# Attention in an order written out for TensorE, ScalarE and VectorE, ahead of two mixtures of experts

## The chip, the core and the metric

The kernel runs on one core of one Trainium2 chip. Five engines work side by side, each through its own queue of instructions, in order: TensorE (PE in the profile) multiplies matrices and transposes, and writes to PSUM alone; VectorE (DVE), ScalarE (ACT) and GpSimd (POOL) work element by element; SyncE (SP) issues the DMA transfers. They meet through semaphores. The metric is the device time of one execution in microseconds (us).

## What is computed

Attention with four batches, eight heads, 1152 keys of 64, where two neighbouring queries are averaged (576 a head), then a mixture of eight experts whose gate is normalised by rows and columns eight times, then a soft mixture with 32 slots. The change is in the attention alone:

```python
def _attn_ref(q, k, v):
    q_pool = q.reshape(B, H, S // 2, 2, D).mean(axis=3)
    scores = (1 / np.sqrt(D)) * np.matmul(q_pool, k.transpose(0, 1, 3, 2))
    scores = scores - np.max(scores, axis=-1, keepdims=True)
    attn = np.exp(scores)
    attn = attn / (np.sum(attn, axis=-1, keepdims=True) + 1e-09)
    return np.matmul(attn, v)
...
    x = attn_out.transpose(0, 2, 1, 3).reshape(B * S, H * D)
    x = _moe_ref(x, ...)
    return _moe2_ref(x, ...)
```

## The kernel before

The attention goes through 16 pairs of heads. A pair has 1152 pooled queries; they make nine tiles of 128, in the order ORDER: first one tile that holds the last 64 queries of both heads (h = 2), then four of head 0 and four of head 1. The loop has one step a tile (NT = 144 tiles; s counts the nine steps of a pair, pi the pairs).

What a tile goes through. emit_SA makes its products with the first 768 keys (SA, two PSUM banks, two buffers) and VectorE takes their maximum (L183); emit_SB does the last 384 keys (SB, one bank, one buffer), the maximum (L191), and the negated maximum of both, nm (L192). emit_exp takes the exp on ScalarE, of SB (L202) and of SA (L203), with the sums on the side. emit_T transposes e in nine chunks of 128 on TensorE: part 0 (four chunks, copied out of PSUM by ScalarE), part 1 (four, by VectorE) and part 2 (the ninth; for the tiles of a head only at every second tile, two chunks at once), into etA, etB or etL. emit_PV multiplies nine chunks of a head by v into the PSUM tile o (one buffer), in two products a chunk (g), which write different halves of the partitions; h = 2 is etL. Every product with v is in full fp32 and stands in the trace as two records. emit_recip inverts the sums, emit_R turns them with transposes (rb, r), and emit_O multiplies o by them into x.

Beside it the next pair is made ready: k_bank transposes k and splits it into a coarse part (ScalarE, L124) and a rest (VectorE, L125), q_bank does the same with q, half after half (L107, L108); kd_dma copies k to both halves of the partitions; pool_q adds query neighbours on GpSimd. All transposes, of e, k, q and the sums, go through two PSUM banks (bank(), pool ps_t), which they use in turn.

In the stage of the attention the order on each engine is set by the framework's scheduler: the loop below gives the program order, and the scheduler lets an instruction that is ready pass one that is not. Products with v are cut by CS in the program into runs of two or three chunks in four steps, and the scheduler cuts them further. The experts after it stand in an order of their own, the program's.

Of the kernel before, what the change touches and what calls it, by code (L numbers as in the profile page):

```python
# [8 lines left out]
F32 = mybir.dt.float32  # L9
F32R = mybir.dt.float32r  # L10
AF = mybir.ActivationFunctionType
# [10 lines left out]
STEPS = len(ORDER)  # L22


def attention(ctx, nc, tc, q, k, v, xa, ident, hooks):
    B, H, S, D = q.shape
    raw_p = ctx.enter_context(tc.tile_pool(name="raw", bufs=2))
    kq_p = ctx.enter_context(tc.tile_pool(name="kq", bufs=1))
    r_p = ctx.enter_context(tc.tile_pool(name="r", bufs=2))
    e_p = ctx.enter_context(tc.tile_pool(name="e", bufs=4))  # L30
    sm_p = ctx.enter_context(tc.tile_pool(name="sm", bufs=4))
    v_p = ctx.enter_context(tc.tile_pool(name="v", bufs=2))
    et_p = ctx.enter_context(tc.tile_pool(name="et", bufs=1))
# [4 lines left out]
    NPAIR = len(pairs)  # L38
# [38 lines left out]
    def pool_q(pi, u):  # L77
        st = prep.setdefault(pi, {})
        if u == 0:
            st["qp"] = kq_p.tile([128, 9, 2, 64], F32, tag="qp", name="qp")  # L80

            st["qs"] = kq_p.tile([128, 1024], F32R, tag="qs", name="qs", bufs=2)
        qr = raws["q"][pi]
        eng = nc.gpsimd if pi else nc.vector
        eng.tensor_tensor(out=st["qp"][:, :, u, :], in0=qr[:, :, 0, :], in1=qr[:, :, 1, :], op=ALU.add)
# [27 lines left out]
    def k_bank(pi, c0, n, ps, at):  # L113
        st = prep.setdefault(pi, {})
        if c0 == 0:
            st["kp"] = kq_p.tile([128, 2, 1152], F32R, tag="kp", name="kp")
        kr = raws["k"][pi]
        for c in range(n):
            nc.tensor.transpose(
                ps[:, at + c * 128:at + (c + 1) * 128], kr[:, c0 + c].rearrange("p h d -> p (h d)"), ident  # L120
            )
        o = st["kp"][:, 0, c0 * 128:(c0 + n) * 128]
        s = ps[:, at:at + n * 128]
        nc.scalar.copy(o, s)  # L124
        nc.vector.tensor_tensor(  # L125
            out=st["kp"][:, 1, c0 * 128:(c0 + n) * 128], in0=s, in1=o.bitcast(F32), op=ALU.subtract
        )
# [34 lines left out]
    NT = len(tiles)  # L162
# [15 lines left out]
    def emit_SA(i):  # L178
        sa = ps_s.tile([128, 2, 512], F32, tag="SA", name="SA", bufs=2)
        for n in range(2):  # L180
            s_mm(i, sa[:, n, :384], n)
        m2 = sm_p.tile([128, 2], F32, tag="m2", name="m2")
        nc.vector.tensor_reduce(out=m2[:, 0:1], in_=sa[:, :, :384], axis=AX.XY, op=ALU.max)  # L183
        S_[i] = (sa, m2)
# [7 lines left out]
        nc.vector.tensor_reduce(out=nm, in_=m2, axis=AX.X, op=ALU.max, negate=True)  # L192
        S_[i] = (sa, sb, nm)

    def emit_exp(i):
        sa, sb, nm = S_.pop(i)
        e = e_p.tile([128, 1152], F32, tag="e", name="e")
        pi, x = divmod(i, STEPS)
        if x == 0:
            sums[pi] = sm_p.tile([128, STEPS, 2], F32, tag="sm", name="sm"), sm_p.tile([128, STEPS], F32, tag="r", name="r")  # L200
        sm = sums[pi][0][:, x]
        nc.scalar.activation(out=e[:, 768:], in_=sb[:, :384], func=AF.Exp, bias=nm, accum_out=sm[:, 0:1])  # L202
        nc.scalar.activation(  # L203
            out=e[:, :768].rearrange("p (n x) -> p n x", n=2), in_=sa[:, :, :384], func=AF.Exp, bias=nm,
            accum_out=sm[:, 1:2],
        )
        E_[i] = e


    def emit_recip(pi, h):  # L210
        sm, r = sums[pi]
        x = slice(5, 9) if h else slice(0, 5)
        nc.vector.scalar_tensor_tensor(
            out=r[:, x], in0=sm[:, x, 0], scalar=1e-9, in1=sm[:, x, 1], op0=ALU.add, op1=ALU.add
        )
        nc.vector.reciprocal(out=r[:, x], in_=r[:, x])
        rb = r_p.tile([128, 2, 2, 64], F32, tag="rb", name="rb")
        nc.gpsimd.tensor_copy(
            rb, r[:, 1 + 4 * h:5 + 4 * h].rearrange("p (g u o) -> p u g o", u=2, o=1).to_broadcast([128, 2, 2, 64])
        )  # L220
        rb_[pi, h] = rb


    def emit_R(pi, h):
        r = sums[pi][1]
        rb = rb_.pop((pi, h))
        ps = bank()
        w = 256
        for u in range(2):
            nc.tensor.transpose(ps[:, 128 * u:128 * u + 128], rb[:, u].rearrange("p g x -> p (g x)"), ident)  # L230
        if h == 0:
            nc.tensor.transpose(ps[:, 256:384], r[:, 0:1].to_broadcast([128, 128]), ident)
            w = 384
        R_[h] = r_p.tile([128, 384], F32, tag="R", name="R")
        nc.scalar.copy(R_[h][:, :w], ps[:, :w])
# [14 lines left out]
    def emit_T(i, part):  # L250
        dst, off = where(i)
        pi, h, t = tiles[i]
        e = E_[i]
        if part < 2:
            c0 = 4 * part
            t_bank([(e, c0 + c) for c in range(4)], dst[:, c0:c0 + 4, off:off + 128], "dve" if part else "act")
            return
        if h == 2:
            t_bank([(e, 8)], dst[:, 8, :], "act")
        elif t % 2:  # L260
            t_bank([(c8.pop((pi, h)), 8), (e, 8)], dst[:, 8, off - 128:off + 128], "act")
        else:
            c8[pi, h] = e

    def emit_PV(pi, h, cs):
        if 0 in cs and h:
            O_[0] = ps_o.tile([128, 512], F32, tag="o", name="o")
        ps = O_[0]
        vr = raws["v"][pi]
        for c in cs:  # L270
            for g in range(2):
                if h < 2:
                    nc.tensor.matmul(  # L273
                        ps[64 * g:64 * g + 64, :256], lhsT=vr[:, h, c, :], rhs=et[h][:, c, 256 * g:256 * g + 256],
                        start=c == 0, stop=c == 8,
                    )
                else:
                    nc.tensor.matmul(
                        ps[64 * g:64 * g + 64, 256:320], lhsT=vr[:, g, c, :], rhs=et[2][:, c, 64 * g:64 * g + 64],
                        start=c == 0, stop=c == 8,  # L280
                    )
# [13 lines left out]
                    in1=R[y, 256 + y.start:256 + y.stop], op=ALU.mult,  # L295
                )

    LAG = 2
    Z = LAG + 4
    CS = [(0, 1), (2, 3), (4, 5), (6, 7, 8)]  # L300
    load_k(0)
    load_q(0)
    for f in (k0, k4):
# [10 lines left out]
    emit_SB(0)  # L314
    q0(0)
    q4(0)
    for i in range(NT + STEPS):
        pi, s = divmod(i, STEPS)
        nxt = pi + 1 if pi + 1 < NPAIR else None
        for f in hooks.get(i - NT, ()):  # L320
            with tc.issue_after(last_dma[0]):
                f()
        j = i - LAG
        if i + 1 < NT:
            emit_SA(i + 1)
        if i < NT:
            emit_exp(i)
            if s in (4, 8):
                emit_recip(pi, int(s == 8))
        if i + 1 < NT:  # L330
            emit_SB(i + 1)
        if nxt is not None:
            prep_at = {0: k0, 2: k4, 4: kq8, 5: q0, 7: q4}
            if s in prep_at:
                prep_at[s](nxt)
            if s == 1:
                pool_q(nxt, 0)
            elif s == 2:
                pool_q(nxt, 1)
        if 0 <= j < NT:  # L340
            emit_T(j, 2)
        if 0 <= j < NT:
            emit_T(j, 0)

        for p, base in ((pi, 0), (pi - 1, STEPS)):
            if 0 <= p < NPAIR:
                z = s + base
                if z == Z:
                    emit_PV(p, 2, range(9))
                elif Z + 1 <= z <= Z + 4:  # L350
                    emit_PV(p, 0, CS[z - Z - 1])
                    if z == Z + 3:
                        emit_R(p, 0)
                    if z == Z + 4:
                        emit_O(p, 0)
                elif Z + 5 <= z <= Z + 8:
                    emit_PV(p, 1, CS[z - Z - 5])
                    if z == Z + 7:
                        emit_R(p, 1)
                    if z == Z + 8:  # L360
                        emit_O(p, 1)
        if 0 <= j < NT:
            emit_T(j, 1)
            E_.pop(j)
        if nxt is not None:
            if s == 4:
                kd_dma(nxt, 0)
            elif s == 6:
                load_v(nxt)
                if nxt + 1 < NPAIR:  # L370
                    load_k(nxt + 1)
                    load_q(nxt + 1)
            elif s == 8:
                kd_dma(nxt, 1)


@with_exitstack
def tile_attention__moe__softmoe(ctx, tc, q, k, v, w_gate, w1, w2, phi, m2_w1, m2_w2, out):
# [134 lines left out]
    with ExitStack() as actx:  # L513
        attention(
            actx, nc, tc, q, k, v, xa, ident,
            {-24: [lambda: stage(0, 0), lambda: split_w(0, 0)],
             -20: [lambda: split_x(0)],
             -12: [lambda: stage(0, 1), lambda: stage(0, 2), lambda: stage(0, 3)],
             -120: [lambda: nc.sync.dma_start(
                 out=wg[:, :, :E], in_=w_gate.rearrange("(k p) e -> p k e", p=128))]},  # L520
        )
# [613 lines left out]
```

## Time and profile before

| what | us |
|---|---|
| median of three runs | 2348.82 |
| lowest, highest | 2347.15, 2455.57 |
| the profiled execution, its time | 2346.86 |
| the profiled execution, its span | 2345.0 |

The span runs from the first to the last instruction of the profile, and the time has 1.9 us around it. TensorE, VectorE, ScalarE and GpSimd were busy 2286.3, 1469.7, 934.0 and 226.2 us of it. Busy time of matmuls is time in which one was anywhere between its start and its end; they overlap, so what a matmul costs is read from the distance of starts. The attention stage fills the first 631 us.

### The profile page before, as it was taken

The page shows a single profiled execution, that of the slowest core. Times are in us where ns is not written, and L with a number is a line of the kernel's source. Part 1 is how long each engine was busy: PE and PEld are TensorE (multiplying, and loading weights), DVE is VectorE, ACT ScalarE, POOL GpSimd, SP SyncE. Part 2 cuts the span into 40 slices and gives each one's busy share as a digit, 9 for nine tenths or more (in the row PEclk, how much of TensorE's full clock was granted, in tenths as well). Part 3 has the DMA queues.
Part 4 walks back from the last instruction along what each step waited for, and adds up shares of the span by engine and source line. Part 5 has one row for each costly group of instructions (what it writes and reads, how often), then busy time and mean ns, then how long its engine had stood idle before and what let it go on. Part 6 is the DMA issues. An engine that isn't in the chain of part 4 may idle for free.

```text
span 2345.0 us, 42628 instructions
## 1 busy us (share of the span) xinstructions
PE 2286.3 (97%) x17797; PEld 2043.3 (87%) x17797; DVE 1469.7 (63%) x2722; ACT 934.0 (40%) x1971; POOL 226.2 (10%) x136
## 2 busy tenths in 40 slices
PE   7999999999999999999999999999999999999996
PEld 5676767777789999999999999999999999988863
DVE  5676667666657686677568558657755865623221
ACT  5666666666543342233234224323332432311211
POOL 1010101000200030021003003002100300100000
PEclk9999999999999999999999999999999999999998
DMA  7444444545121222122112112112111221221169
GB/s 184 106 117 123 109 112 102 117 95 124 42 81 64 82 73 81 55 73 82 59 60 90 64 46 100 58 60 81 66 71 64 73 81 55 89 110 55 55 221 309
DMA packets 119918, 216.20 MB, mean 92 GB/s; under 512 B 43440, under 2 KB 95152, under 8 KB 106416
## 3 DMA queue, kind: packets, MB, share of 16 engines
q1 hardware_dynamic: 119728, 213.49, 30.1%
q8 instruction: 141, 2.31, 0.4%
q14 instruction: 49, 0.40, 0.1%
HBM read 161.56 MB, written 14.16 MB: 75 GB/s over the span
## 4 chain that ended last, share of the span: by engine, by line
PE 82%; issue 8%; DVE 7%; DMA 1%; ACT 1%; SPq 0%; POOL 0%; DVEq 0%; ACTq 0%; POOLq 0%
PE g L565 9%; PE g L566 9%; PE g L567 9%; PE o L273 8%; PE t L240 7%; PE y L594 7%; PE y L592 7%; PE y L593 7%; PE SA L174 5%; PE SB L174 2%; DVE ho L554 2%; DVE ht L547 2%; PE y L664 1%; DVE v L486 1%; PE y L666 1%
## 5 line engine op out<-in xcount | busy, mean ns | idle before, releaser
L565 PE MATMUL g<-xs,w 128*128 128x256 f32 x2304 | 660.1, 286 | 0.0
L566 PE MATMUL g<-xs,w 128*128 128x256 f32 x2304 | 654.3, 284 | 0.0
L567 PE MATMUL g<-xs,w 128*128 128x256 f32 x2304 | 654.1, 284 | 0.2 <-DVE w L461 0.2
L592 PE MATMUL y<-v,ho 128*128 128x256 f32 x1764 | 503.1, 285 | 9.0 <-ACT ho L553 9.0
L594 PE MATMUL y<-v,ho 128*128 128x256 f32 x1764 | 503.1, 285 | 7.1 <-DVE ho L554 7.1
L593 PE MATMUL y<-v,ho 128*128 128x256 f32 x1764 | 502.0, 285 | 0.0
L581 ACT ACTIVATE hr<-g 128x512 f32<-128x512 f32 x252 | 150.4, 597 | 770.6 <-PE g L567 754.5
L565 PEld LDWEIGHTS g<-xs,w 128*128 128x128 f32 x2304 | 445.0, 193 | 7.7 <-issue 7.4
L566 PEld LDWEIGHTS g<-xs,w 128*128 128x128 f32 x2304 | 444.8, 193 | 0.3
L567 PEld LDWEIGHTS g<-xs,w 128*128 128x128 f32 x2304 | 444.5, 193 | 0.4 <-DVE w L461 0.4
L547 DVE TENSOR_TENSOR ht<-hr 128x512 f32<-128x512 f32 x315 | 230.1, 764 | 223.7 <-ACT hr L581 221.3
L592 PEld LDWEIGHTS y<-v,ho 128*128 128x128 f32 x1764 | 340.9, 193 | 10.3 <-ACT ho L553 10.3
L594 PEld LDWEIGHTS y<-v,ho 128*128 128x128 f32 x1764 | 341.6, 194 | 8.5 <-DVE ho L554 8.5
L593 PEld LDWEIGHTS y<-v,ho 128*128 128x128 f32 x1764 | 341.2, 193 | 0.0
L602 DVE SCALAR_TENSOR_TENSOR acc<-y,P,acc 128x256 f32<-128x256 f32 x540 | 244.6, 478 | 117.4 <-PE y L594 117.4
L554 DVE TENSOR_TENSOR ho<-ht,ho 128x512 fp32r<-128x512 f32 x315 | 258.8, 822 | 6.9 <-ACT ho L553 6.9
L553 ACT CAST ho<-ht 128x512 fp32r<-128x512 f32 x315 | 188.9, 618 | 81.2 <-DVE ht L547 78.6
L240 PE MATMUL t<-ident,e 128*128 128x128 f32 x1296 | 205.4, 281 | 1.4 <-ACT etL L244 0.6
L240 PEld LDWEIGHTS t<-ident,e 128*128 128x128 f32 x1296 | 144.9, 140 | 64.7 <-issue 23.1
L461 POOL TENSOR_TENSOR w<-stg,w 128x1024 fp32r<-128x1024 f32 x28 | 68.0, 2429 | 1193.3 <-ACT w L460 1193.3
L183 DVE TENSOR_REDUCE m<-SA 128x1 f32<-128x768 f32 x144 | 137.8, 957 | 61.5 <-PE SA L174 60.5
L554 DVE TENSOR_TENSOR ho<-hr,ho 128x512 fp32r<-128x512 f32 x126 | 97.5, 774 | 55.8 <-ACT ho L553 55.8
(187 smaller groups left out, 2732.0 us busy)
## 6 DMA issues: line engine op xcount, KB each, us to landing
xs<-xd SPq DMA_DIRECT2D x63, 1024.0 KB, 4.8
kd<-kp SPq DMA_DIRECT2D x64, 576.0 KB, 6.9
stg<-in_moe_w_dram SPq DMA_DIRECT2D x60, 512.0 KB, 5.8
m2w<-in_moe_w_dram SPq DMA_DIRECT2D x13, 1024.0 KB, 9.4
m2w<-in_moe_w_dram SPq DMA_DIRECT2D x22, 512.0 KB, 8.7
kr<-in_k_dram SPq DMA_DIRECT2D x32, 288.0 KB, 4.7
qr<-in_q_dram SPq DMA_DIRECT2D x16, 576.0 KB, 6.7
vr<-in_v_dram SPq DMA_DIRECT2D x16, 576.0 KB, 4.3
```

Source lines behind the costliest of these rows:

```text
L240: nc.tensor.transpose(ps[:, 128 * x:128 * x + 128], src[:, c * 128:(c + 1) * 128], ident)
L273: nc.tensor.matmul(ps[64 * g:64 * g + 64, :256], lhsT=vr[:, h, c, :], rhs=et[h][:, c, 256 * g:256 * g + 256], start=c == 0, stop=c == 8,)
L547: nc.vector.tensor_tensor(out=src, in0=q[0], in1=q[1], op=op)
L553: nc.scalar.copy(o[:, 0], src)
L554: nc.vector.tensor_tensor(out=o[:, 1], in0=src, in1=o[:, 0].bitcast(F32), op=ALU.subtract)
L565: nc.tensor.matmul(o, lhsT=w[:, 0, kk, c], rhs=x[:, 0, kk], start=kk == 0, stop=False)
L566: nc.tensor.matmul(o, lhsT=w[:, 0, kk, c], rhs=x[:, 1, kk], start=False, stop=False)
L567: nc.tensor.matmul(o, lhsT=w[:, 1, kk, c], rhs=x[:, 0, kk], start=False, stop=kk == 3)
L592: nc.tensor.matmul(ps, lhsT=o[:, 0, c], rhs=v[:, 0, c], start=c == 0, stop=False)
L593: nc.tensor.matmul(ps, lhsT=o[:, 0, c], rhs=v[:, 1, c], start=False, stop=False)
L594: nc.tensor.matmul(ps, lhsT=o[:, 1, c], rhs=v[:, 0, c], start=False, stop=c == 3)
L602: nc.vector.scalar_tensor_tensor(out=y, in0=ps, scalar=p, in1=y, op0=ALU.mult, op1=ALU.add)
```

## The change

On TensorE, ScalarE and VectorE the order of the program is now the order of execution in the attention too (manual_schedule with these three). The loop is written anew: the step of tile i takes the exp of i in two parts, transposes the tile before (i - 1) around it, makes SB of the next tile and SA of the one after that, and does one thing besides, X: a run of three chunks of products with v (all nine for etL), the split of a piece of the next k or q, or the transposes of the sums. Queues of GpSimd and SyncE stay with the scheduler. r goes from two buffers to one, e from four to three, kp from one to two. The first load and split of the experts' weights are asked for at other steps. What is computed is the same.

```diff
--- before.py
+++ after.py
...
-    r_p = ctx.enter_context(tc.tile_pool(name="r", bufs=2))
-    e_p = ctx.enter_context(tc.tile_pool(name="e", bufs=4))
+    r_p = ctx.enter_context(tc.tile_pool(name="r", bufs=1))
+    e_p = ctx.enter_context(tc.tile_pool(name="e", bufs=3))
...
-            st["kp"] = kq_p.tile([128, 2, 1152], F32R, tag="kp", name="kp")
+            st["kp"] = kq_p.tile([128, 2, 1152], F32R, tag="kp", name="kp", bufs=2)
...
-    def emit_exp(i):
-        sa, sb, nm = S_.pop(i)
...
+    def emit_exp(i, part):
+        sa, sb, nm = S_[i]
         pi, x = divmod(i, STEPS)
+        if part:
+            sm = sums[pi][0][:, x]
+            nc.scalar.activation(
+                out=E_[i][:, :768].rearrange("p (n x) -> p n x", n=2), in_=sa[:, :, :384], func=AF.Exp, bias=nm,
+                accum_out=sm[:, 1:2],
+            )
+            S_.pop(i)
+            return
...
+        nc.scalar.activation(out=E_[i][:, 768:], in_=sb[:, :384], func=AF.Exp, bias=nm, accum_out=sm[:, 0:1])
...
+    def X(pi, s):
+        nxt = pi + 1 if pi + 1 < NPAIR else None
+        on = pi < NPAIR
+        if s == 0:
+            if nxt is not None:
+                k0(nxt)
+            if pi:
+                emit_R(pi - 1, 0)
+        elif s < 4:
+            if pi:
+                emit_PV(pi - 1, 1, range(3 * s - 3, 3 * s))
+        elif s == 4:
+            if nxt is not None:
+                k4(nxt)
+            if pi:
+                emit_R(pi - 1, 1)
+        elif s == 5:
+            if on:
+                emit_PV(pi, 2, range(9))
+            if nxt is not None:
+                kq8(nxt)
+        else:
+            if on:
+                emit_PV(pi, 0, range(3 * s - 18, 3 * s - 15))
+            if nxt is not None and s > 6:
+                (q0 if s == 7 else q4)(nxt)
+
+    def loads(pi, s):
...
+        if s == 3:
+            pool_q(nxt, 0)
+        elif s == 4:
+            pool_q(nxt, 1)
+        elif s == 5:
+            kd_dma(nxt, 0)
+        elif s == 6:
+            load_v(nxt)
...
+        elif s == 8:
+            kd_dma(nxt, 1)
+
+    ET = mybir.EngineType
+    ctx.enter_context(tc.manual_schedule(engines={ET.PE, ET.Activation, ET.DVE}))
...
+    emit_SA(1)
+    for i in range(NT + 5):
         pi, s = divmod(i, STEPS)
...
+        if pi:
+            if s == 1:
+                emit_O(pi - 1, 0)
+            elif s == 0:
+                emit_recip(pi - 1, 1)
+        j = i - 1
+        on = 0 <= j < NT
         if i < NT:
+            emit_exp(i, 0)
+        if on:
+            emit_T(j, 0)
         if i + 1 < NT:
             emit_SB(i + 1)
+        if i < NT:
+            emit_exp(i, 1)
+        if on:
+            emit_T(j, 1)
+        X(pi, s)
+        if on:
             emit_T(j, 2)
             E_.pop(j)
+        if i + 2 < NT:
+            emit_SA(i + 2)
+        if s == 5 and i < NT:
+            emit_recip(pi, 0)
+        if s == 4 and pi:
+            emit_O(pi - 1, 1)
+        loads(pi, s)
...
-            {-24: [lambda: stage(0, 0), lambda: split_w(0, 0)],
+            {-28: [lambda: stage(0, 0)],
+             -24: [lambda: split_w(0, 0)],
```

What moves, word for word in the order of the built programs, at three places. TensorE around the step in which a pair ends or begins and head 1 is multiplied by v, before (L240 transposes e, L90 q, L119 k, L230 and L232 the sums; L273 multiplies by v, etB being the transposed e of head 1; kd is the copied k):

```order
L240 MATMUL t<-ident,e 128x128 x2
L273 MATMUL o<-etB,vr 64x256 x3
L240 MATMUL t<-ident,e 128x128 x4
L90 MATMUL t<-ident,qp 128x128
L273 MATMUL o<-etB,vr 64x256
L174 MATMUL SA<-kd_3044,qs 128x384 x4
L174 MATMUL SB<-kd_3044,qs 128x384 x2
L273 MATMUL o<-etB,vr 64x256
L230 MATMUL t<-ident,rb 128x128 x2
L273 MATMUL o<-etB,vr 64x256 x2
L240 MATMUL t<-ident,e 128x128 x4
L90 MATMUL t<-ident,qp 128x128 x4
```

and after (L244 transposes e, L234 and L236 the sums; L277 multiplies by v):

```order
L244 MATMUL t<-ident,e 128x128 x4
L174 MATMUL SB<-kd_1686,qs 128x384 x2
L244 MATMUL t<-ident,e 128x128 x4
L119 MATMUL t<-ident,kr 128x128 x4
L234 MATMUL t<-ident,rb 128x128 x2
L236 MATMUL t<-ident,sm 128x128
L244 MATMUL t<-ident,e 128x128 x2
L174 MATMUL SA<-kd_1686,qs 128x384 x4
L244 MATMUL t<-ident,e 128x128 x4
L174 MATMUL SB<-kd_1686,qs 128x384 x2
L244 MATMUL t<-ident,e 128x128 x4
L277 MATMUL o<-etB,vr 64x256 x6
```

Before, products with v (o) stand in runs of three, one, one and two, between pieces of other work; after, none stand in the step that begins a pair, then six in a row, and transposes stand ahead of and behind each SB.

ScalarE between the last split of q and the next tile's exp, before (L202 and L203 are the exps of SB and SA, L107 the halves of q):

```order
L202 ACTIVATE e,sm<-SB,nm 128x384
L203 ACTIVATE e,sm<-SA,nm 128x768
L107 ACTIVATE qs<-t 128x256
L244 COPY etB<-t 128x4x128
L107 ACTIVATE qs<-t 128x256
L202 ACTIVATE e,sm<-SB,nm 128x384
L203 ACTIVATE e,sm<-SA,nm 128x768
L244 COPY etB<-t 128x256
L244 COPY etB<-t 128x4x128
```

and after (L211 and L200 are the exps, L239 copies the sums R):

```order
L200 ACTIVATE e,sm<-SA,nm 128x768
L107 ACTIVATE qs<-t 128x256 x2
L211 ACTIVATE e,sm<-SB,nm 128x384
L248 COPY etB<-t 128x4x128
L200 ACTIVATE e,sm<-SA,nm 128x768
L124 CAST kp<-t 128x512
L239 COPY R<-t 128x384
L248 COPY etB<-t 128x256
L211 ACTIVATE e,sm<-SB,nm 128x384
```

Before, the two exps of a tile stand ahead of the first half, and a copy stands between the halves; after, the halves follow each other, and the next tile's exp of SB stands behind both. At the pair's change the k cast, R's copy and the last chunk's copy stand ahead of that exp.

VectorE at the change from one pair to the next, before (L108 is the rest of q, L183, L191 and L192 the maxima, L213 and L216 sum and reciprocal):

```order
L108 SCALAR_TENSOR_TENSOR qs<-t,qs 64x256
L244 COPY etB<-t 128x4x128
L183 TENSOR_REDUCE m_3008<-SA 128x1
L213 SCALAR_TENSOR_TENSOR r<-sm 128x4
L191 TENSOR_REDUCE m_3008<-SB 128x1
L216 RECIPROCAL r<-r 128x4
L192 TENSOR_REDUCE nm<-m_3008 128x1
L244 COPY etB<-t 128x4x128
```

and after (L217 and L220 are sum and reciprocal, L248 the copy out of a transposes' bank):

```order
L108 SCALAR_TENSOR_TENSOR qs<-t,qs 64x256 x2
L183 TENSOR_REDUCE m_2653<-SA 128x1
L217 SCALAR_TENSOR_TENSOR sm<-sm 128x4
L220 RECIPROCAL sm<-sm 128x4
L191 TENSOR_REDUCE m_2653<-SB 128x1
L192 TENSOR_REDUCE nm<-m_2653 128x1
L248 COPY etB<-t 128x4x128
L125 TENSOR_TENSOR kp<-t,kp 128x512
```

Before, the maximum of SB stands between sum and reciprocal; after, both rests of q, the maximum of SA, sum and reciprocal all stand ahead of the maximum of SB, and the copy that frees the bank behind it.

## Rows read from the trace of the kernel before

**Rows 1.** The page of the kernel before: busy time of TensorE (PE) over the whole span with its share and the number of instructions, and the clock that was granted to it, in tenths, over 40 equal slices of the span.

```profile
PE 2286.3 (97%) x17797; PEld 2043.3 (87%) x17797; DVE 1469.7 (63%) x2722; ACT 934.0 (40%) x1971; POOL 226.2 (10%) x136
...
PEclk9999999999999999999999999999999999999998
```

**Rows 2.** The view by windows, the stretch 60 to 600 us in the attention stage: length, busy time of TensorE, its weight loads (PEld), VectorE (DVE), ScalarE (ACT) and GpSimd (POOL) with the number of instructions, then granted clock, DMA share and GB/s.

```profile
60.00:600.00 540.00, 540.00 (x3806) 382.47 (x3806) 371.84 (x782) 340.15 (x868) 47.55 (x54) 1.00 0.46 110
```

**Rows 3.** The timeline of TensorE: the S products of the shared tile, which come once in a pair, in the pairs that start at 87 and at 583 us. Columns: start, length, engine, line, operation, tiles, shape, count.

```profile
87.08 1.29 PE L174 MATMUL SA<-kp,qd 128*128 128x384 f32 x6
...
583.21 1.29 PE L174 MATMUL SA<-kp,qd 128*128 128x384 f32 x6
```

**Rows 4.** The timeline again (same columns, merged runs), three places of the stage: t are transposes, SA and SB the products of q and k, o the products with v (etB, etA, etL), two records to a product.

```profile
303.67 0.65 PE L273 MATMUL o<-etB,vr 128*64 128x256 f32 x2
304.24 0.44 PE L230 MATMUL t<-ident,rb 128*128 128x128 f32 x2
...
505.28 0.60 PE L90 MATMUL t<-ident,qp 128*128 128x128 f32 x4
...
505.71 0.60 PE L240 MATMUL t<-ident,e 128*128 128x128 f32 x4
...
506.24 1.08 PE L273 MATMUL o<-etA,vr 128*64 128x256 f32 x8
...
507.26 0.66 PE L240 MATMUL t<-ident,e 128*128 128x128 f32 x4
...
606.36 1.51 PE L273 MATMUL o<-etB,vr 128*64 128x256 f32 x12
607.81 0.66 PE L240 MATMUL t<-ident,e 128*128 128x128 f32 x4
608.22 0.94 PE L174 MATMUL SA<-kd,qs 128*128 128x384 f32 x4
609.00 0.51 PE L174 MATMUL SB<-kd,qs 128*128 128x384 f32 x2
609.35 0.94 PE L240 MATMUL t<-ident,e 128*128 128x128 f32 x6
610.22 1.27 PE L278 MATMUL o<-etL,vr 128*64 128x64 f32 x36
611.42 0.65 PE L240 MATMUL t<-ident,e 128*128 128x128 f32 x4
```

**Rows 5.** Groups by line and form, 60 to 600 us: line, engine, operation, tiles, shapes, count, then busy time and mean length of one in ns, then the idle time ahead of them and what ended it.

```profile
L244 ACT COPY etB<-t 128x256 f32<-128x256 f32 x29 | 10.8, 372 | 44.1 <-PE t L240 44.1
...
L108 DVE SCALAR_TENSOR_TENSOR qs<-t,qs 64x256 fp32r<-64x256 f32 x56 | 23.9, 426 | 9.4 <-ACT qs L107 8.9
...
L244 DVE COPY etB<-t 128x512 f32<-128x512 f32 x57 | 39.3, 690 | 16.4 <-PE t L240 15.4
...
L124 ACT CAST kp<-t 128x128 fp32r<-128x128 f32 x14 | 3.7, 266 | 2.7 <-PE t L119 1.8
...
L125 DVE TENSOR_TENSOR kp<-t,kp 128x128 fp32r<-128x128 f32 x14 | 3.5, 254 | 0.0
...
L213 DVE SCALAR_TENSOR_TENSOR r<-sm 128x4 f32<-128x4 f32 x14 | 2.3, 166 | 0.4
...
L216 DVE RECIPROCAL r<-r 128x4 f32<-128x4 f32 x14 | 2.4, 170 | 0.0
```

**Rows 6.** The timeline of all engines, two places: near 25 us, where TensorE waited for an exp, and near 505 us, where the next instruction of the same engine starts at once.

```profile
25.22 0.15 DVE L192 TENSOR_REDUCE nm<-m 128x1 f32<-128x2 f32 x1
25.41 0.58 ACT L202 ACTIVATE e<-SB,nm 128x384 f32<-128x384 f32 x1 [1.21 <-DVE nm L192]
...
26.14 0.61 PE L174 MATMUL SB<-kd,qs 128*128 128x384 f32 x2 [0.30 <-ACT e L202]
...
505.13 0.96 DVE L183 TENSOR_REDUCE m<-SA 128x1 f32<-128x768 f32 x1
...
506.00 0.55 DVE L191 TENSOR_REDUCE m<-SB 128x1 f32<-128x384 f32 x1
...
507.04 0.39 ACT L107 ACTIVATE qs<-t 128x256 fp32r<-128x256 f32 x1
...
507.32 0.58 ACT L202 ACTIVATE e<-SB,nm 128x384 f32<-128x384 f32 x1
```

**Rows 7.** The timeline at the end of the attention stage: the first exp of the last tile, and the last multiplications that write x.

```profile
614.52 0.58 ACT L202 ACTIVATE e<-SB,nm 128x384 f32<-128x384 f32 x1 [0.34 <-DVE nm L192]
...
625.32 0.46 DVE L293 TENSOR_TENSOR x<-o,R 64x64 f32<-64x64 f32 x2
...
630.05 0.86 DVE L290 TENSOR_TENSOR x<-o,R 64x256 f32<-64x256 f32 x2 [3.56 <-PE o L273]
```

**Rows 8.** The view by windows for a stretch near 42 us and two stretches at the turn of an expert (columns as in rows 2), and two rows of TensorE's timeline inside the first of them.

```profile
41.70:45.10 3.40, 2.96 (x20) 2.12 (x18) 3.33 (x5) 1.26 (x3) 0.00 (x0) 1.00 0.91 237
...
1062.30:1065.70 3.40, 1.72 (x12) 1.31 (x12) 3.37 (x5) 2.23 (x4) 0.58 (x1) 1.00 0.39 132
1065.80:1069.10 3.30, 3.30 (x18) 3.30 (x18) 3.30 (x7) 2.65 (x4) 0.00 (x0) 0.52 0.00 0
...
43.18 0.44 PE L240 MATMUL t<-ident,e 128*128 128x128 f32 x2
43.90 1.10 PE L240 MATMUL t<-ident,e 128*128 128x128 f32 x8 [0.28 <-DVE etA L244]
```

More of the change, by code (lines that the diff above doesn't have):

```diff
@@ L193, in emit_SB @@
         S_[i] = (sa, sb, nm)
-    def emit_exp(i):
-        sa, sb, nm = S_.pop(i)
-        e = e_p.tile([128, 1152], F32, tag="e", name="e")
+    def emit_exp(i, part):
+        sa, sb, nm = S_[i]
         pi, x = divmod(i, STEPS)
+        if part:
[6 more added lines that the diff above has]
+            return
+        E_[i] = e_p.tile([128, 1152], F32, tag="e", name="e")
         if x == 0:
-            sums[pi] = sm_p.tile([128, STEPS, 2], F32, tag="sm", name="sm"), sm_p.tile([128, STEPS], F32, tag="r", name="r")
+            sums[pi] = [sm_p.tile([128, STEPS, n], F32, tag=f"sm{n}", name="sm") for n in (2, 1)]
+            sums[pi][1] = sums[pi][1].rearrange("p s o -> p (s o)")
         sm = sums[pi][0][:, x]
[L202 to L207, printed above, removed]
+        nc.scalar.activation(out=E_[i][:, 768:], in_=sb[:, :384], func=AF.Exp, bias=nm, accum_out=sm[:, 0:1])
     def emit_recip(pi, h):
@@ L296, in emit_O @@
                 )
-    LAG = 2
-    Z = LAG + 4
-    CS = [(0, 1), (2, 3), (4, 5), (6, 7, 8)]
+    def X(pi, s):
[25 more added lines that the diff above has]
+    def loads(pi, s):
+        nxt = pi + 1
+        if nxt >= NPAIR:
+            return
+        if s == 3:
[6 more added lines that the diff above has]
+            load_v(nxt)
+            if nxt + 1 < NPAIR:
+                load_k(nxt + 1)
+                load_q(nxt + 1)
+        elif s == 8:
+            kd_dma(nxt, 1)
+    ET = mybir.EngineType
+    ctx.enter_context(tc.manual_schedule(engines={ET.PE, ET.Activation, ET.DVE}))
     load_k(0)
@@ L316, in attention @@
     q4(0)
-    for i in range(NT + STEPS):
+    emit_SA(1)
+    for i in range(NT + 5):
         pi, s = divmod(i, STEPS)
-        nxt = pi + 1 if pi + 1 < NPAIR else None
         for f in hooks.get(i - NT, ()):
@@ L322, in attention @@
                 f()
-        j = i - LAG
-        if i + 1 < NT:
-            emit_SA(i + 1)
+        if pi:
[5 more added lines that the diff above has]
+        on = 0 <= j < NT
         if i < NT:
-            emit_exp(i)
-            if s in (4, 8):
-                emit_recip(pi, int(s == 8))
+            emit_exp(i, 0)
+        if on:
+            emit_T(j, 0)
         if i + 1 < NT:
             emit_SB(i + 1)
[L332 to L340, printed above, removed]
-            emit_T(j, 2)
[L342 to L363, printed above, removed]
-            E_.pop(j)
[L365 to L374, printed above, removed]
+        if i < NT:
[4 more added lines that the diff above has]
+        if on:
+            emit_T(j, 2)
+            E_.pop(j)
+        if i + 2 < NT:
[5 more added lines that the diff above has]
+        loads(pi, s)
 @with_exitstack
```

## The prediction, on record before the changed kernel ran

> **What bounds the kernel now.** I read the busy shares first, then the stage that the change touches, then TensorE's order in time, then the ends of the stage. TensorE is busy 97% of the span, at full granted clock nearly throughout [rows 1]. In the attention stage (60 to 600 us) it is busy 540.00 of 540.00 us, VectorE 69%, ScalarE 63% [rows 2]: the stage is TensorE's issue time, with room on the other two. A pair of heads takes (583.21 - 87.08)/13 = 38.16 us [rows 3]; there are 16. After the last O at 630.9 come the experts, which the change leaves alone: 2345.0 - 630.9 = 1714 us [rows 7] as before.
>
> "Busy" hides what matmuls cost, so I price them by the starts of neighbours [rows 4]. Four transposes take 0.43, 0.109 each. Six S matmuls take 1.13: 0.174 each, and 0.08 that the transposes before them give back. A product with v is two records, and two products with different g overlap: a run of 8 records (two slots) takes 1.02, one of 12 (three slots) 1.45; that is 0.43 a slot and 0.15 a run. Half a slot is no cheaper: a single product took 0.57. A run also costs its neighbours: four transposes that lead into it take 0.53 instead of 0.43, and those behind it stand 0.66 instead of 0.60. So a visit to the o tile costs 0.15 + 0.10 + 0.06, about 0.30, beside its slots. The 36 records of etL took 1.20 for 9 slots, 0.117 each.
>
> **What the change takes away.** The orders give the counts. Before: 242 runs of o and 49 of etL; 136 and 34 of them have an odd length and leave half a slot empty; 356 and 161 slots. After: 94 and 16 runs, none odd; 288 and 144 slots. For a pair:
> before: 104 transposes 11.3, 57 S 9.9, 22.3 o slots 9.6, 10.1 etL slots 1.2, 18.2 visits 5.5, sum 37.5 against 38.16 measured; the prices hold to 2%.
> after: 11.3 + 9.9 + 18 slots 7.8 + 9 slots 1.0 + 7 visits 2.1 = 32.1.
> If nothing else moved, that would be 16 x (37.5 - 32.1) = 86 us less.
>
> **What it adds: waits.** Now nothing overtakes on three engines. A waiting instruction holds all behind it, and what TensorE needs back soon (a bank of ps_t, the one SB bank) stands on ScalarE and VectorE behind other work. I walk one pair, steps 0 to 8, with durations from [rows 5, 6], hops of 0.03 to 0.05 between engines ([rows 6]: nm ended 25.37, exp began 25.41), 0.15 from the end of an exp to the SB it frees (25.99 to 26.14), and the issue time where the next may start before the end: 0.87 of the big maximum's 0.96, 0.28 of a q half's 0.39, some 0.1 off a copy.
>
> Step 8 to 0, SB behind the q halves. ScalarE does half of q, VectorE its rest, ScalarE the other half, and only then the next tile's first exp. From the end of the last q transpose: 0.04 + 0.38 + 0.03 + 0.43 + 0.03 + 0.28 + 0.58 + 0.15 = 1.92. TensorE goes on 0.17 before that end with SA (0.78) and four transposes (0.35), and is ready after 0.9: **wait 1.0**. Before, copies and exps stand between the halves, and TensorE has a run of o.
> Step 0, R's bank. R needs the bank that VectorE's copy of the second four transposes frees. VectorE's chain from the second q rest, 0.16 after the exp's start: 0.45 + 0.87 (SA maximum) + 0.29 (sum and reciprocal, the second behind the first) + 0.58 (SB maximum) + 0.07 + 0.69 + 0.05, so 3.16. TensorE, late by the wait above, wants it at 0.73 + 0.43 + 0.44 + 0.44 = 2.04: **1.1**. Then the last chunk waits for k's rest in its bank: **0.3**.
> Step 1. The exp stands behind the last chunk's copy (0.04 + 0.27 + 0.58 + 0.15 = 1.04 against SA and four transposes, 0.89): **0.15**. The new o run stands behind four multiplications of O, which came after SA's maximum: 0.04 + 0.87 + 0.43 + 0.44 + 0.46 + 0.05 = 2.3 from SA's end against 1.3: **1.0**.
> Steps 2, 3 and 7: none. The parts of x and w that are now split inline fall into steps 3 and 7, where ScalarE waits for TensorE; I price them at nothing (1.2 us each if that is wrong).
> Step 4. The exp behind R's copy **0.15**. R's bank, without the reciprocals: 0.61 (SB) + 0.04 + 0.55 + 0.03 + 0.07 + 0.69 + 0.05 = 2.04 against 1.31: **0.7**.
> Step 5. The exp **0.15**; the etL run behind two multiplications, 0.04 + 0.87 + 0.86 + 0.05 = 1.8 against 1.3: **0.5**; q's ninth transpose shares k's bank and waits for k's cast and rest, 0.28 + 0.04 + 0.27 + 0.03 + 0.25 + 0.05 = 0.92 against 0.16: **0.76**.
> Steps 5 to 6 and 7 to 8. The q halves stand ahead of the last chunk's copy, which frees the next transposes' bank, and that ahead of the exp: **0.33 + 0.21** and **0.51 + 0.21**.
> Sum 7.1. The pair then takes 32.1 + 7.1 = 39.2 against 38.16, **1.0 more**, 16 x 1.0 = 17 us in all. If the 0.7 by which my prices fell short of before stays in after, 11 us more; I take half, 6.
>
> Ends. Before, 16.4 us lie between the last tile's first exp (614.5) and the last O (630.9) [rows 7]; after, the old order's last four steps are gone, and two runs of products, two of R and their waits leave about 11.5: 5 less. The start loses 2 to 3, since the first pair's splits no longer overtake. Together -3. The buffer counts cost nothing: an e is read one step after its exp, so three do, and kp's two let k be split while SA of the old pair is read. The kd transfers are issued in steps 5 and 8, three and four steps (over 11 us) ahead of their use; priced at nothing; a late one costs what it lacks, once a pair. GpSimd is busy 47.55 of 540 us [rows 2], so its additions for q, asked for two steps later and needed in step 5, stay covered.
>
> **Clock.** [...] I expect this to catch two or three of 16 pairs, at up to 1.7 us (half of 3.4): 4 us.
> [...]
>
> Sum, on the profiled execution of 2346.9 us (span 2345.0; the median of three is 2348.8): 2346.9 + 17 + 6 - 3 + 4 = 2371; I say **2370 us**, 0.9% up.
>
> **Rivals.**
> (1) The waits are covered and TensorE runs at its issue time: 16 x (32.1 + 0.7 - 38.2) = -86, 2261 us. For it: VectorE and ScalarE have a third of their time free [rows 2]. Against it: the waits come from the order of dependent pieces, not from load. Over 2% faster needs waits under 2.8 a pair, 40% of my sum. 0.07.
> (2) Slower, by the clock. If each pair falls to the lower level twice, in step 0 and around steps 5 to 6 (1.8 of 5 us waiting), that is 16 x 2 x 1.7 = 54 on top: 2366 + 54 = 2420 us. It decides from the point where most pairs fall twice; one fall a pair gives 2393, still within 2%. For it: TensorE would wait a sixth of a stage in which it never waited. Against it: the stretch that fell in [rows 8] was half idle, which I find in step 0 alone. 0.08.
> (3) [...] 0.03.
> [...]
> That the runs are not joined is no case: after's order shows six in a row.
>
> **How the numbers follow.** Forecast 0.82, rivals 0.07, 0.08 and 0.03. A quarter more or less in the waits is 16 x 1.75 = 28 us each way: 2342 to 2398. That holds single falls of the clock too; the rivals beyond stay out. 2% (47 us) is about what a measurement of this kernel can tell from no change. Faster by more 0.07, within it 0.82, slower by more 0.11.
>
> **What would show it.** Runs of 12 records of L277 at 1.45 each; TensorE no longer 540 of 540 but some 85% busy in the stage; waits of about 1 us, once a pair each, of SB on the exp of SB (L211), of R on VectorE's copy (L248) and of the o run on O; a pair in 39 to 40 us. A pair under 37 with these waits in it means that the issue prices are wrong. [...]

## The result, and the profile after

The changed kernel takes **2379.8 us** (2377.4 to 2380.4) against 2349.0: a ratio of 1.0132, 95% interval 1.0112 to 1.0152, so slower by 1.3%: under the 2% that was set out above as a difference that tells, with an interval clear of 1. One of the four runs of the kernel before, 2455.6 us, is over 4% above the others and stands outside the ratio. The profiled execution took 2380.2 us, span 2378.3, 33.3 more than before.

The page of the changed kernel answers to [rows 1]: busy time by engine, TensorE's clock over the span, and the chain that ended last by engine.

```profile
PE 2238.5 (94%) x17797; PEld 2036.8 (86%) x17797; DVE 1474.8 (62%) x2722; ACT 936.9 (39%) x1971; POOL 226.1 (10%) x136
...
PEclk9999999999999999999999999999999999999997
...
PE 73%; DVE 13%; issue 9%; ACT 3%; DMA 1%; SPq 0%; POOL 0%; DVEq 0%; ACTq 0%; POOLq 0%
```

TensorE has as many instructions as before and is busy 48 us less, in a span that is 33 us longer. Where it stands still is seen in the stretch 60 to 600 us of the view by windows (columns as in [rows 2]).

```profile
60.00:600.00 540.00, 470.05 (x3599) 356.18 (x3598) 355.97 (x736) 324.68 (x818) 46.93 (x53) 1.00 0.43 102
```

It was busy 540 of 540; now 470, at a granted clock of 1.00 in the mean. VectorE and ScalarE are a little less busy than before, since the pairs are longer: the lost 70 us are not their load. The pair, from the S products of the shared tile as in [rows 3]:

```profile
90.01 1.29 PE L174 MATMUL SA<-kp,qd 128*128 128x384 f32 x6
...
210.94 1.29 PE L174 MATMUL SA<-kp,qd 128*128 128x384 f32 x6
```

(210.94 - 90.01)/3 = 40.31 us against 38.16. The view of waits says what TensorE waited for in the same stretch (its line, tile and what released it; us in total, times, longest):

```profile
PE t L234 <- DVE etB L248: 14.5, 13, 1.1
PE o L277 <- DVE x L297: 12.1, 14, 0.9
PE SB L174 <- ACT e L211: 10.1, 13, 0.8
PE t L234 <- DVE etA L248: 9.4, 13, 0.7
PE t L90 <- DVE kp L125: 8.9, 13, 0.7
PE o L282 <- DVE x L294: 6.9, 13, 0.5
```

Each comes 13 or 14 times in 13.4 pairs, so once a pair. They add to 62 of the 70 us. In the timeline (columns as in [rows 4], idle time and its releaser at the end) three of them stand in steps 8 to 1 of a pair:

```profile
297.57 0.60 PE L244 MATMUL t<-ident,e 128*128 128x128 f32 x4
298.94 0.61 PE L174 MATMUL SB<-kd,qs 128*128 128x384 f32 x2 [0.78 <-ACT e L211]
...
299.83 0.60 PE L119 MATMUL t<-ident,kr 128*128 128x128 f32 x4
301.55 0.41 PE L234 MATMUL t<-ident,rb 128*128 128x128 f32 x2 [1.12 <-DVE etB L248]
...
303.98 0.60 PE L244 MATMUL t<-ident,e 128*128 128x128 f32 x4
305.47 1.51 PE L277 MATMUL o<-etB,vr 128*64 128x256 f32 x12 [0.88 <-DVE x L297]
...
309.15 1.51 PE L277 MATMUL o<-etB,vr 128*64 128x256 f32 x12
310.60 0.97 PE L174 MATMUL SA<-kd,qs 128*128 128x384 f32 x4
```

The idle time counts from the modelled end of the last matmul; from start to start less the price, the first wait is 298.94 - 297.57 - 0.43 = 0.94. The joined run at the end takes 310.60 - 309.15 = 1.45, as priced in [rows 4]. The end of the stage, with [rows 7]:

```profile
652.01 0.59 ACT L211 ACTIVATE e<-SB,nm 128x384 f32<-128x384 f32 x1
...
663.04 0.86 DVE L294 TENSOR_TENSOR x<-o,R 64x256 f32<-64x256 f32 x2 [5.02 <-ACT R L239]
```

The last tile's first exp comes 37.5 us later than before; from it to the last O it is 11.9 us, not 16.4. The experts behind take what they took (1714.5 for 1714.1). The clock fell once inside a steady pair, to 0.50 for 3.4 us (view by windows):

```profile
338.50:341.90 3.40, 1.54 (x11) 1.29 (x12) 3.12 (x8) 2.65 (x7) 1.70 (x2) 1.00 0.21 39
341.90:345.30 3.40, 3.40 (x14) 3.25 (x15) 1.26 (x2) 1.38 (x5) 0.40 (x1) 0.50 0.34 134
```

It is step 0 of a pair, behind the waits of SB and R. That pair took 41.39, so the fall cost 1.1 us. Between 20 and 30 us, in the first pair, the granted clock stood at 0.50 too, from 21.0 us for 6.9 us, which it did not do in the kernel before (its row first, then that of the changed kernel):

```profile
20.00:30.00 10.00, 8.86 (x36) 7.20 (x34) 6.67 (x13) 5.53 (x14) 0.00 (x0) 1.00 1.05 277
...
20.00:30.00 10.00, 8.26 (x39) 7.18 (x38) 6.25 (x11) 5.68 (x15) 0.00 (x0) 0.66 1.07 272
```

### The profile page after: what moved, and what is told of

Its sections match the earlier page's. It is cut to its first block, busy times and chain, and to the rows that moved or that the text cites. A ratio compares the mean times of both kernels' runs of the same rounds, so it can differ in the third digit from the quotient of the medians.

```text
span 2378.3 us, 42570 instructions
## 1 busy us (share of the span) xinstructions
PE 2238.5 (94%) x17797; PEld 2036.8 (86%) x17797; DVE 1474.8 (62%) x2722; ACT 936.9 (39%) x1971; POOL 226.1 (10%) x136
## 4 chain that ended last, share of the span: by engine, by line
PE 73%; DVE 13%; issue 9%; ACT 3%; DMA 1%; SPq 0%; POOL 0%; DVEq 0%; ACTq 0%; POOLq 0%
PE g L592 9%; PE g L593 9%; PE g L594 9%; PE y L621 7%; PE y L619 7%; PE y L620 7%; PE o L277 6%; PE t L244 4%; PE SA L174 3%; DVE m L183 2%; DVE ho L581 2%; DVE ht L574 2%; PE SB L174 2%; PE y L691 1%; DVE v L512 1%
## 5 line engine op out<-in xcount | busy, mean ns | idle before, releaser
L244 PE MATMUL t<-ident,e 128*128 128x128 f32 x1296 | 206.8, 277 | 10.0 <-ACT etB L248 4.9
L183 DVE TENSOR_REDUCE m<-SA 128x1 f32<-128x768 f32 x144 | 137.9, 958 | 117.9 <-PE SA L174 116.5
L244 PEld LDWEIGHTS t<-ident,e 128*128 128x128 f32 x1296 | 157.6, 141 | 45.7 <-issue 11.9
```

The source lines that it names most:

```text
L244: nc.tensor.transpose(ps[:, 128 * x:128 * x + 128], src[:, c * 128:(c + 1) * 128], ident)
```

## Experiments

Theory A is that of the prediction: the joined runs save what they were priced at, and what is lost are single waits, each from one piece of ScalarE's or VectorE's work that a fixed order puts ahead of what TensorE wants. Its rivals: B, the two engines' work sets the pace and the order only decides where a wait shows; C, the new order on TensorE, with transposes one tile behind exp, is the cause; D, joined runs save less than priced. The expectations call the scheduler the planner, and the way of adding up a pair that the prediction used the walk. Measured values (a pair is one in which the clock did not fall; the kernel before has pairs of 37.5 to 39.0, and its figure is their mean; a ratio with interval where the kernel was timed in rounds, else the time of one run, with that of the kernel before on the same chip beside it):

| kernel | pair | time, us | against before |
|---|---|---|---|
| before | 38.16 | 2349.0 | |
| after | 40.31 | 2379.8 | 1.0132 (1.0112 to 1.0152) |
| oearly | 38.75 | 2355.0 | 1.0031 (1.0019 to 1.0043) |
| kq8 | 40.05 | 2383.4 | 2347.5 |
| rbank | 39.94 | 2372.8 | 2347.7 |
| qhalf | 40.51 | 2387.5 | 2347.7 |
| four | 38.11 | 2351.8 | 1.0016 (1.0006 to 1.0026) |
| cut | 42.54 | 2409.7 | 2347.5 |
| peonly | 38.77 | 2358.2 | 1.0043 (1.0027 to 1.0060) |
| peact | 38.90 | 2353.8 | 2345.6 |
| pedve | 40.40 | 2386.0 | 2345.6 |
| man2 | 40.40 | 2384.8 | 2343.3 |
| joined | 37.83 | 2346.1 | 2343.3 |
| free | 37.34 | **2331.7** | **0.9941 (0.9924 to 0.9958)** |

**One piece moved: O (oearly).**

```diff
+        if pi and s in (0, 4):
+            emit_O(pi - 1, s // 4)
         if i + 2 < NT:
             emit_SA(i + 2)
```

(and the two calls of emit_O where they stood are gone)

> The multiplications that write O (L297, L294) are issued ahead of the next SA's maximum on VectorE, not behind it; nothing else moves. In the changed kernel's trace the o run waits 0.88 us and the etL run 0.54 us a pair behind them. Theory A (the loss is made of single waits, each from one piece that stands in the wrong place of a fixed order): both waits go, the pair falls from 40.31 to about 38.9, the run from 2380 to about 2357. Theory B (ScalarE and VectorE together set the pace, the order only decides where the wait shows): the same time turns up in front of S or R, the pair stays within 0.3 of 40.31, 2375 to 2380.

Measured: pair 38.75, 1.56 less; 2355.0. Both waits on x are gone from the view of waits, and the others stand as they did:

```profile
PE t L234 <- DVE etB L248: 14.4, 13, 1.1
PE SB L174 <- ACT e L211: 10.8, 14, 0.8
PE t L234 <- DVE etA L248: 10.1, 14, 0.7
PE t L90 <- DVE kp L125: 9.5, 14, 0.7
```

Theory B falls: VectorE does the same work in a shorter pair. Four fifths of the time lost hung on the place of six instructions a pair.

**The ninth block (kq8).** q's transpose is issued ahead of k_bank's cast and rest.

```diff
         ps = bank()
+        q_turn(pi, 8, 1, ps, 128)
         k_bank(pi, 8, 1, ps, 0)
-        q_bank(pi, 8, 1, ps, 128)
+        q_bank(pi, 8, 1, ps, 128, True)
```

> Both transposes of the ninth block (k's and q's, one shared bank) are issued ahead of the casts and rests that read the bank, so q's no longer waits for VectorE's k rest (0.68 us a pair after). Theory A says that the wait goes, but behind it stand four transposes that wait for ScalarE's copy, which is late by the same chain, so most of it is given back: pair 40.1, 3 us less in all (2377). If the 0.68 goes whole: 39.6, 2369. Theory B: 40.3.

Measured: 40.05, as expected: the wait on kp is gone, and the next four transposes, L249 here, wait for ScalarE's copy instead, as the view of waits has it (3.8 us in all before this edit):

```profile
PE t L249 <- ACT etA L253: 11.8, 13, 0.9
```

But its one run was 3.6 us longer than the changed kernel. In nine pairs in a row the clock fell in step 0; these take 40.97, 0.92 more each. One of them, by windows:

```profile
137.50:140.90 3.40, 1.58 (x11) 1.22 (x10) 3.00 (x8) 2.77 (x7) 1.82 (x2) 1.00 0.22 52
140.90:144.30 3.40, 3.33 (x14) 3.23 (x15) 1.23 (x2) 1.37 (x4) 0.40 (x1) 0.50 0.33 130
```

2383.4 - 9 x 0.92 = 2375 is an estimate of what the order alone would give, a gain of some 4.

**The price of a visit (cut).**

```diff
-                emit_PV(pi - 1, 1, range(3 * s - 3, 3 * s))
+                emit_PV(pi - 1, 1, range(3 * s - 2, 3 * s))
...
+        if 0 < s < 4 and pi:
+            emit_PV(pi - 1, 1, range(3 * s - 3, 3 * s - 2))
         if on:
             emit_T(j, 1)
```

(and the same for the runs of the other head)

> The 12-record runs of products with v are cut in two, 4 records ahead of the third four transposes' place and 8 where they were: the same products and slots, 6 visits more a pair to the o tile. By the prediction's price (0.30 us a visit, half of it seen only in neighbours) the pair grows by about 1.9 and TensorE's waits are partly shortened by being later: 42 to 42.5, run 2408 to 2414. Rival D (the visit price is wrong and the long runs save little): 40.3 to 40.7, 2380 to 2387.

Measured: 42.54, 2.23 more. One wait grew with it, from 12.1/14 = 0.86 to 16.8/13 = 1.29:

```profile
PE o L277 <- DVE x L297: 16.8, 13, 1.3
```

2.23 - 0.43 = 1.80 for six visits: 0.30 each, the price that was worked out. Rival D falls.

**R's bank (rbank).** In steps 0 and 4 the last lines of emit_SB, the maximum of SB and nm, become a function that is called behind emit_T(j, 1).

> In steps 0 and 4 VectorE copies the second four transposes (whose bank R waits for, 1.1 and 0.7 us) before the maximum of SB, not behind it. Theory A, by the walk with the new order: R waits 0.8 less in step 0, but SB's maximum, and with it the next exp and what is freed by that, comes 0.7 later, so that most is taken back; pair 40.0, 4 to 5 us less in all (2375). If both R waits shrank by VectorE's 0.6 maximum and nothing took it back: 39.1, 2361. Theory B: 40.3.

Measured: 39.94. R's wait in step 0 fell from 1.1 to 0.5, and a wait for ScalarE's copy of R came up behind it:

```profile
PE t L248 <- ACT R L243: 7.4, 13, 0.6
...
PE t L238 <- DVE etB L252: 5.9, 13, 0.5
```

**The second half of q (qhalf).** Its two instructions are put on a list, which is issued behind the next exp of SB.

```diff
+        if h and pi:
+            later.append(a)
...
             emit_exp(i, 0)
+        while later:
+            split(*later.pop(0))
```

> The second half of each q split is issued behind the next exp of SB instead of ahead of it (both engines), so that exp, and the SB that waits for it in step 0 (1.0 us), no longer stand behind it. Theory A: 0.6 to 0.7 off the pair, 39.6 to 39.7, 2369 to 2371. Theory B: 40.3.

Measured: 40.51, a miss by 0.85. SB's wait is gone as expected, but k's transposes wait 1.1 for the second q rest. The timeline shows why; L225 is the sum of the row sums (L217 in the changed kernel), L116 the q rest, L85 an addition on GpSimd (two in the row):

```profile
300.30 2.78 POOL L85 TENSOR_TENSOR qp<-qr 128x576 f32<-128x576 f32 x2 [10.77 <-PE t L90]
300.66 0.43 DVE L116 SCALAR_TENSOR_TENSOR qs<-t,qs 64x256 fp32r<-64x256 f32 x1 [1.43 <-ACT qs L115]
...
302.09 1.01 DVE L225 SCALAR_TENSOR_TENSOR sm<-sm 128x4 f32<-128x4 f32 x1
...
303.35 0.43 DVE L116 SCALAR_TENSOR_TENSOR qs<-t,qs 64x256 fp32r<-64x256 f32 x1
...
303.83 0.66 PE L127 MATMUL t<-ident,kr 128*128 128x128 f32 x4 [1.13 <-DVE qs L116]
```

The sum, 0.17 in the changed kernel (below), takes 1.01 here, and ends 0.02 behind GpSimd's end (300.30 + 2.78 = 303.08); so in each of the 14 pairs in which GpSimd runs beside it. The q rest runs beside GpSimd at its 0.43. Why the one is drawn out and the other is not, no run shows. In the changed kernel the sum starts when GpSimd has 0.1 us left, and takes its 0.17:

```profile
299.79 0.17 DVE L217 SCALAR_TENSOR_TENSOR sm<-sm 128x4 f32<-128x4 f32 x1
```

Without the 0.84 the pair would be 39.67, what theory A had expected; that is an estimate, no run of this move has the sum elsewhere. The clock also fell in every second pair, 0.85 each.

**All four (four).**

> All four moves together: O ahead of SA's maximum, both transposes of the ninth block first, the copy that frees R's bank ahead of SB's maximum, the second q half behind the next exp. The walk with these orders gives 3.0 less a pair, more than the sum of the single moves (1.5 + 0.2 + 0.3 + 0.7 = 2.7), since a wait that one move hands on is taken by another: pair 37.3, run 2332 to 2340, under the kernel before by 0.5%. Theory B (what ScalarE and VectorE can do in a pair is the limit, O just happened to stand badly): no more than the move of O alone, 38.7, 2355. If the moves stand in each other's way: 39 or more, 2360.

Measured: 38.11 and 1.0016, on a level with the kernel before but not under it. Theory B's bound (38.7) is passed, and the miss of 0.8 has the size of the sum's delay, which is there again: 1.00 to 1.05 in 14 pairs, ending with GpSimd. The clock fell in four pairs (in one to 0.50 from 138.2 to 141.6 us), which took 1.4 more in three cases and 1.8 in one. The order with the sum moved away from GpSimd's addition was not tried; 38.1 - 0.85 = 37.3 is an estimate.

**Which engine's order (peonly, peact, pedve).** One edit, the set of engines that are held to the written order:

```diff
-    ctx.enter_context(tc.manual_schedule(engines={ET.PE, ET.Activation, ET.DVE}))
+    ctx.enter_context(tc.manual_schedule(engines={ET.PE}))
```

> The written order holds for TensorE alone (the same order there as in the changed kernel); ScalarE's and VectorE's instructions are placed by the planner again, which lets ready work overtake. Theory A: half to two thirds of the waits of some 8 us a pair stay, since single pieces still stand ahead of what TensorE wants; pair about 38.5, 2352 to 2360. Rival C (the order on TensorE itself is the cause, transposes one tile behind exp leave it too little to do between a product and its exp): pair 40 or more, 2375 or more. If the waits all come from the fixed order on ScalarE and VectorE: pair near 33, 2265.

> TensorE and ScalarE are held to the written order, VectorE's instructions are placed by the planner. Theory A: VectorE's fixed order is the one that costs (O ahead of what the next product waits for, SB's maximum ahead of the copy for R): pair 38.7, 2354. If ScalarE's fixed order costs as much: 39.5, 2367.

> TensorE and VectorE are held to the written order, ScalarE's instructions are placed by the planner. Theory A, as for the run with VectorE free: VectorE's order stays and its waits stay, only SB's wait behind the q halves (1.0 us) can go, and VectorE's copies hand part of it on: pair 40.1, 2377. If ScalarE's order is the one that costs: 38.7, 2354.

Measured: 38.77, 38.90 and 40.40 (the last 0.3 over what was expected). Releasing VectorE gives all the gain there is in releasing both, 1.4 a pair; releasing ScalarE alone gives none (in pedve the clock fell in nine pairs besides, 0.978 in the mean of its run where the changed kernel has 0.984, so its time has more in it than the order). Of the two engines it is **VectorE's** fixed order that costs, and moving O alone (oearly, 38.75) gave back as much. With TensorE alone held, 60 us of waits are left in the stretch, spread over more places:

```profile
60.00:600.00 540.00, 480.10 (x3733) 363.46 (x3735) 359.91 (x764) 329.28 (x848) 47.31 (x54) 1.00 0.45 108
```

**Transposes two tiles behind (man2).** emit_T takes j = i - 2, R, O and the products come a step later, e has four buffers, kp one.

> The three engines are held to a written order as in the changed kernel, but the transposes stand two tiles behind exp, as before the change, and with them R, O and the products one step later; e has four buffers again, and kp one. If one tile of distance is too little and makes the waits (rival C): they shrink, pair 38.5 or less, 2351. Theory A (waits of ScalarE's and VectorE's order): the same pieces stand ahead of the same banks, the walk finds 0.2 more than for one tile, pair 40.5, 2383.

Measured: 40.40. The distance is not the cause, and rival C falls as far as it rests on it; what the holding of TensorE costs is read from the next run.

**The new order, held nowhere (free).** The line of manual_schedule is taken out.

> The program is written in the new order, but no engine is held to it: the planner places TensorE, ScalarE and VectorE as before the change. On TensorE the 110 runs of products become 158 (62 of them odd; 291 and 170 before the change) and 463 slots instead of 432 (517 before). By the prices: 1.9 slots and 3.0 runs a pair more than in the changed kernel, 0.8 + 0.9, so 34 us of issue; the walk of that order finds half the waits of the fixed one, 3.6 a pair. Theory A (what the change loses is what nothing may overtake, what it gains are joined runs): pair 37.0 to 38.0, run 2328 to 2345, faster than both. If the longer runs are what the change really pays for (rival D) or the new place of the transposes is what costs (rival C): 38.7 or more, 2356 or more.

Measured: 37.34 and 0.9941: **faster than both kernels**, than the one before by 0.6%. The pair, and windows and waits:

```profile
84.90 1.29 PE L174 MATMUL SA<-kp,qd 128*128 128x384 f32 x6
...
458.35 1.29 PE L174 MATMUL SA<-kp,qd 128*128 128x384 f32 x6
...
60.00:600.00 540.00, 515.38 (x3913) 382.45 (x3913) 374.53 (x796) 344.41 (x885) 48.73 (x55) 1.00 0.47 111
...
PE SB L174 <- ACT e L211: 9.6, 15, 0.7
PE t L244 <- ACT R L239: 7.2, 13, 0.6
PE t L234 <- DVE etB L248: 6.8, 13, 1.5
```

(458.35 - 84.90)/10 is the pair. 25 us of standing still are left of 70. Against peonly, 38.77, the pair is 1.4 shorter: holding TensorE to the written order costs as much as holding VectorE to it. Some runs are split again, but 158 are far fewer than the 291 before the change; by the prices that is what puts the pair under the 38.16 of the kernel before, in which nothing stood still.

**The cut of the chunks alone (joined).** In the kernel before:

```diff
-    CS = [(0, 1), (2, 3), (4, 5), (6, 7, 8)]
+    CS = [(), (0, 1, 2), (3, 4, 5), (6, 7, 8)]
```

> The kernel before with one edit: the nine chunks of each product with v are written as three runs of three, as in the change, not as 2, 2, 2 and 3, and left to the planner. The planner takes them apart again (255 runs, 186 odd; 291 and 170 before). Theory A (the new order as a whole, not the cut of the chunks, gives the planner longer runs): 36 visits less and 8 slots more, 0.5 less a pair, 37.7, 2340 at best, and not the 37.3 of the new order left to the planner. If the cut alone is the gain: 37.3, 2333.

Measured: 37.83 (37.93 as a mean over the same 13 pairs as before's 38.16), between the two, and 2346.1 in one run beside 2343.3 of the kernel before: the 0.2 to 0.3 a pair does not show in the whole. In its profile the first pair is 1.6 us longer than before, and the clock fell twice in it (0.985 in the mean of the run, 0.986 for the kernel before). So the cut of the chunks alone does not give the gain of the free run. What the buffer counts and the other places of the weights' loads give was not tried by itself.

## Why the prediction was right, and by how much it was short

The forecast was 2370 us and slower by 0.9%, it is 2379.8 and 1.3%, inside the range and by the mechanism named. Against the profiled execution of before the sum said 24 us, the trace 33.3. Step by step:

- **Issue time, 32.1 a pair.** The terms hold: runs of 12 at 1.45, a visit 0.30 (cut). 40.31 less the waits below is 32.7; so the 0.7 by which the prices fell short of before stays nearly whole, where half was taken.
- **Waits, 7.1 a pair.** Every one was in its place, and the mechanism is shown: moving one piece took its wait away and left the others (oearly). From start to start less the price, in the pair of the rows above, predicted and found: SB 1.0 and 0.94; R 1.1 and 1.28; the last chunk 0.3 and 0.15; exp in steps 1, 4 and 5 0.15 and 0.14 each; o run 1.0 and 0.96; R in step 4 0.7 and 0.88; etL 0.5 and 0.70; q's ninth 0.76 and 0.90; steps 5 to 6 0.54 and 0.66; 7 to 8 0.72 and 0.73. Found: 7.6. Short were the chains over three hops (R, etL, q's ninth), by 0.14 to 0.20 each.
- The pair was thus put at 39.2 + 0.4 = 39.6 and is 40.31; the 0.7, times 16, is the term that was mis-sized: 34.4 us of pairs where 23 stood. The pair of "39 to 40 us" that was named as a sign is missed by 0.3.
- **Ends.** 4.5 gained behind the last exp (5 predicted), 2.0 lost at the start (2 to 3 predicted), which is what the other terms leave: the first exp comes 1.5 later (19.70 for 18.22), the rest lies in the first pair. -2.5 in all for -3. The fall of the clock there was not foreseen, and little of it shows: from the first exp to the tenth the changed kernel takes 36.7, and rbank, whose clock stood at 1.00 there, 36.8. The splits that now stand inline were put at nothing; a pair in which one of them stands is 0.35 longer (40.66).
- **Clock.** One steady pair fell, at 1.1 us, for two or three at up to 1.7; 4 us stood for 1. It was in step 0. No run shows the term of 4 us, or 1.7 a fall: beside the 1.1 here, falls in the other runs took 0.46 to 1.45, and in two cases 1.8 and 2.1. 34.4 - 2.5 + 1.1 = 33.0 of the 33.3. That the clock was put 3 too high hid a part of the 11 by which the pairs were put too low; so much of the nearness is luck.
- **Rival 1** (waits covered) fails in the changed kernel, and comes nearest where nothing is held: 37.34, not 32.8, since the scheduler splits runs again and waits remain. **Rival 2**: falls in step 0 of nine pairs were seen in kq8, but once a pair and at 0.9, not twice at 1.7; a fall behind the waits of step 5 was seen once (peonly). **Rival 3** (0.03) falls: in the changed kernel transposes fill steps 0, 4 and 5 of a pair, and the clock was 1.00 in the mean from 60 to 600 us, with one fall in a steady pair. (In the stretch of [rows 8] near 42 us, with 14 transposes among its 20 matmuls, it was 1.00 too.)
- "GpSimd's additions stay covered" held for the additions, and left out what runs beside them: VectorE's sum, which takes its 0.17 in the changed kernel, and 0.84 more a pair in qhalf and four, where it begins a microsecond earlier against them.

## What to carry to other kernels

When an order is fixed by hand on an engine that still had time to spare, walk one period of it: for each thing that the bounding engine wants back, add up what stands ahead of it on the engine that gives it. Here the walk found each wait to 0.2 us, and showed a cheap repair, six instructions moved for 25 us (16 pairs at 1.56). And split the change: of the 3.0 us a pair between the changed kernel and the free one, holding VectorE to the written order cost 1.4 and holding TensorE to it 1.4, and the new program without the holding beat both kernels.

## What the runs showed of the hardware that was not expected

A VectorE sum over 128x4 elements, 0.17 us, took 1.01 when it began beside a GpSimd addition of 128x576 with 1 us left, and ended 0.02 us behind it. The granted clock fell in step 0 of nine pairs in a row in kq8 and in no pair of rbank, where R waits 1.1 and 0.5 us in that step; kq8's pairs without a fall have the 1.1 too, so what sets a fall off is not shown. In the two falls that are shown, of the changed kernel and of kq8, TensorE was busy for 1.54 and 1.58 of the 3.4 us ahead. The fall of the changed kernel lasted 3.4 us at 0.50, and a fall did not cost the half of that, 1.7: pairs with one took 0.46 (pedve) to 1.45 us (four) more than the others of their kernel. In two cases more was lost, 1.8 (four) and 2.1 (peonly); in the second a wait on kp was also longer by 0.5, which does not account for all of it.
